# Attention and a squared-ReLU feed-forward on one core: three quarters of the up tiles in seven block products, two merged unit queues, banks taken late

## The chip, the cores and the metric

The kernel runs on one core of one Trainium2 chip. The metric is the device time of one execution in microseconds, taken as the median of several runs. A core has a matrix engine (PE in the profile; its weight loads are the separate row PEld), a vector engine (DVE), a scalar engine (ACT), a general engine (POOL) and a queue engine (SP); they run their own instruction streams in order and meet at semaphores.

## What is computed

Eight batches of grouped-query attention (16 query heads, 4 key/value heads, 384 tokens, head size 64) give 3072 tokens of width 1024. They go through a feed-forward block of width 2048 with a squared ReLU.

```python
batch, n_q_heads, n_kv_heads, seq, head_dim = (8, 16, 4, 384, 64)
scores = scale * np.matmul(q, k.transpose(0, 1, 3, 2))
attn = np.exp(scores)
attn = attn / (np.sum(attn, axis=-1, keepdims=True) + 1e-09)
attn_out = np.matmul(attn, v)
x = attn_out.transpose(0, 2, 1, 3).reshape(B * S, H * D)   # 3072 x 1024
h = np.maximum(x @ w_in, 0.0)                              # w_in 1024 x 2048
out = h * h @ w_out                                        # w_out 2048 x 1024
```

## The kernel before

A Python program writes out the instruction streams of all engines. `Recorder.add` (line 53) puts one operation on one engine, derives its semaphore waits from the names of what it reads and writes, and keeps an assumed start and end for it. From those assumed times the loop at lines 1109 to 1159 decides what TensorE does next. So the order on each engine is fixed before the launch, and an engine whose next instruction isn't ready simply stands.

The matrix array is used as two halves of 64 rows. A `Piece` (line 453) is one matmul over 64 rows, and two pieces on different halves run side by side. A unit of work is all pieces of the lower half followed, from the point that `hold_back` (line 465) sets, by all pieces of the upper half into the same PSUM bank. Four banks serve the feed-forward work (`F_BANKS`, line 501), three the scores, and one, `po`, the attention output.

The work of a batch has these kinds of unit:

- Scores (`row_scores`, line 512): for each pair of heads six matmuls of 384 columns, three to one exponential on ACT (line 524) into one of three `expT` buffers.
- Attention output (`row_attend`, line 535): 36 matmuls of 65 columns into `po`, then a reciprocal and a multiplication on DVE (lines 548 and 550) into `o_sb`, and a DMA transpose (`put_x`, line 433) into one of three `xT` buffers.
- Up tile (`row_up`, line 623): 128 of the 2048 hidden features for the 384 tokens of a batch. Eight pieces of 384 columns on each half, a ReLU on DVE (line 641) into one of three `hr` buffers, a square on ACT (line 649) into `h2T`. Sixteen tiles a batch, one after the other.
- Down products: the first two blocks of 128 tokens are plain (`row_down`, line 677). All others go in pairs of 128-token blocks, and each pair is done in seven products in place of eight (`product`, line 756; `p1` to `p3`, `rest`): sums of weight blocks are made once (`w_sums`, line 710), sums of activation blocks for every pair on DVE (`a_sums`, line 735). Product 1 and 2, and 5 and 3, share a PSUM bank and add up there.

The feed-forward is one stream of units (`feed_forward`, line 949: the up tiles of a batch, then its down pairs), and the attention another; the loop mixes them by a pace per batch (`PACE`, line 1006). Inputs of the next batch are loaded by POOL (`load_k`, `load_q`, `load_v`, lines 207 to 222): k and v land in `k_st` and `v_st`, POOL copies k twice into `k_dup` (line 354) and v into `v_aug` (line 383), and SP issues DMA transposes of k and q (`turn_k` and `turn_q`, lines 360 to 374).

```python
161 NEX, NXT, NHR, NY, NO, NS = 3, 3, 3, 6, 4, 5
592 ((load_k, 62000.0), (load_q, 67000.0), (load_v, 68500.0))
```

Line 161 holds the buffer counts; line 592 the assumed landing times of the third batch's loads, in ns, which the planner uses for that batch alone.

Of the kernel before, what the change touches and what calls it, by code (L numbers as in the profile page):

```python
# [9 lines left out]
class Recorder:  # L10
# [6 lines left out]
    def __init__(self, nc):  # L17
        self.nc = nc
        self.ops = []
        self.writer = {}  # L20
        self.readers = {}
        self.dma_sems = {}
        self.dma_last = {}
        self.idle_at = dict.fromkeys(self.ENGINES, 0.0)
        self.rows_at = [0.0, 0.0]
        self.stalled = {}
# [3 lines left out]

    def needs(self, eng, reads, writes, dma=None, after=()):
        deps = set()
# [9 lines left out]
        for d in deps:  # L42
            o = self.ops[d]
            if o["dma"] is None and o["eng"] == eng and dma is None:
                if eng in self.IN_ORDER or d not in raw:
                    continue
            need.add(d)
# [5 lines left out]
    def add(self, eng, fn, reads=(), writes=(), dma=None, after=(), ns=500.0, lat=2200.0, rows=None, end=None):  # L53
        i = len(self.ops)
        need = self.needs(eng, reads, writes, dma, after)
# [81 lines left out]
def bass_gqa_attention__then__ffn_squared_relu_kernel(  # L137
# [23 lines left out]
    NEX, NXT, NHR, NY, NO, NS = 3, 3, 3, 6, 4, 5  # L161

    R = Recorder(nc)

# [4 lines left out]
    warm = sb("warm", [128, 256])  # L169
# [10 lines left out]
    k_st = sb("k_st", [128, HKV, NJ, D])  # L180
    v_st = sb("v_st", [128, HKV, NJ, D])
    k_dup = [a_late[:, 0:2 * NKV].rearrange("p (a x d) -> p a x d", a=HKV * NJ, x=2), sb("k_dup1", [128, HKV * NJ, 2, D]).ap()]
    EARLY_W = [("q_f", c) for c in range(NPB)] + [("k_f", g) for g in range(HKV)] + ["v_f"] + [("q_st", 0, c) for c in range(NPB)]
    EARLY_A = [("k_dup", 0, g, j) for g in range(HKV) for j in range(NJ)]
    q_st = [q_b0, q_next.ap()]
    v_aug = [sb(f"v_aug{i}", [128, HKV * NJ, D + 1]) for i in range(2)]
    kT = [sb(f"kT{i}", [128, HKV, S]) for i in range(2)]
    qT = [sb(f"qT{i}", [128, NPB, S]) for i in range(2)]
    expT = [sb(f"expT{i}", [128, 2 * NJ, S]) for i in range(NEX)]
    rinv = [sb(f"rinv{i}", [128, NJ, 2], f32) for i in range(2)]  # L190
    o_sb = [sb(f"o_sb{i}", [128, NJ, 2, D]) for i in range(NO)]
    xT = [sb(f"xT{i}", [128, NKC, S]) for i in range(NXT)]
    w_in_sb = sb("w_in_sb", [128, NKC, FF], f16)
    w_out_sb = sb("w_out_sb", [128, NFC, F], f16)
    hr = [sb(f"hr{i}", [128, S], f32) for i in range(NHR)]
    h2T = [sb(f"h2T{i}", [128, NFC, S]) for i in range(2)]
    y_sb = [sb(f"y_sb{i}", [128, F // 2], f32) for i in range(NY)]

# [8 lines left out]
    def load_k(b, after=(), end=None):  # L207
        R.add("gpsimd", lambda g: g.dma_start(
            k_st.ap().rearrange("p g j d -> p g (j d)"),
            k[b].rearrange("g (p j) d -> p g (j d)", j=NJ)),  # L210
            writes=["k_st"], dma="k", after=after, ns=900.0, lat=LOADS, end=end)

    def load_v(b, after=(), end=None):
        R.add("gpsimd", lambda g: g.dma_start(
            v_st.ap().rearrange("p g j d -> p g (j d)"),
            v[b].rearrange("g (p j) d -> p g (j d)", j=NJ)),
            writes=["v_st"], dma="v", after=after, ns=900.0, lat=LOADS, end=end)
# [9 lines left out]
    def load_w_in(i):  # L227
        R.add("gpsimd", lambda g: g.dma_start(
            w_in_sb[:, :, i * WC:(i + 1) * WC],
            moe_w_in[:, i * WC:(i + 1) * WC].rearrange("(c p) f -> p c f", p=128)),  # L230
            writes=[("w_in", i)], dma=f"wi{i}", end=20500.0 + 2700.0 * i)
# [13 lines left out]
    def first_q(c0, c1):  # L245
# [14 lines left out]
    R.add("vector", lambda e: e.memset(warm[:], 0.0), writes=["warm"])  # L260
# [3 lines left out]
        pattern=[[-1, 128]], channel_multiplier=1), reads=["ident"], writes=["ident"])  # L264
    for i in range(2):
# [6 lines left out]
    def dup_k(g, eng, j0=0, j1=NJ):  # L272
        src = k_f[:, g, j0:j1].unsqueeze(2).to_broadcast([128, j1 - j0, 2, D])
        R.add(eng, lambda e: e.tensor_copy(k_dup[0][:, g * NJ + j0:g * NJ + j1], src),
              reads=[("k_f", g)], writes=[("k_dup", 0, g, j) for j in range(j0, j1)])
# [43 lines left out]
    def turn_bank(banks):  # L319
        i = banks[slots[0] % len(banks)]  # L320
        slots[0] += 1
        if i >= 5:
            return f_ps[i - 5].ap().bitcast(bf16)[:, 0:S], ("f_ps", i - 5)
        return sc_bf[:, i, 0:S], ("sc", i)

    def turn_on_pe(src, src_keys, dst, dst_keys, banks, eng="vector", n=NJ):
        ps, key = turn_bank(banks)

        def tr(pe):
            for t in range(n):  # L330
                m = pe.matmul(ps[:, t * 128:(t + 1) * 128], src[:, t * 128:(t + 1) * 128], ident[:],  # L331
# [3 lines left out]
        R.add("tensor", tr, reads=[*src_keys, "ident"], writes=[key])  # L335
# [4 lines left out]

    def first_kT(g, b=0, banks=RING, j0=0, j1=NJ):
        turn_on_pe(k_dup[b][:, g * NJ + j0:g * NJ + j1].rearrange("p a x d -> p (a x d)"),
                   [("k_dup", b, g, j) for j in range(j0, j1)], kT[b][:, g, j0 * 128:j1 * 128],
                   [("kT", b, g, j) for j in range(j0, j1)], banks, n=j1 - j0)

    def first_qT(c, b=0, banks=RING):
        turn_on_pe(q_st[b][:, 2 * c:2 * c + 2, :].rearrange("p h e -> p (h e)"), [("q_st", min(b, 1), c)],
                   qT[b][:, c], [("qT", b, c)], banks)

    def first_oT(c, banks=RING, eng="vector"):  # L350
        turn_on_pe(o_sb[c % NO].ap().rearrange("p i s d -> p (i s d)"), [("o_sb", c % NO, x) for x in range(2)],
                   xT[0][:, c], [("xT", 0, c)], banks, eng)

    def dup_all_k(b, eng="vector"):
        src = k_st.ap().rearrange("p g j d -> p (g j) d").unsqueeze(2)
        R.add(eng, lambda e: e.tensor_copy(
            k_dup[1][:, :, :, :], src.to_broadcast([128, HKV * NJ, 2, D])),
            reads=["k_st"], writes=[("k_dup", 1, g, j) for g in range(HKV) for j in range(NJ)], ns=1500.0)

    def turn_k(b, g):  # L360
        gs = slice(g * NJ, (g + 2) * NJ)
        R.add("sync", lambda e: e.dma_start_transpose(
            kT[b % 2][:, g:g + 2].rearrange("p g (j c) -> p (g j) c", j=NJ),
            k_dup[1][:, gs].rearrange("p a x d -> p (a x d)")),
            reads=[("k_dup", 1, x, j) for x in (g, g + 1) for j in range(NJ)],
            writes=[("kT", b % 2, x, j) for x in (g, g + 1) for j in range(NJ)], dma=f"kt{b % 2}_{g}", ns=1250.0)

    def turn_q(b, c):
        cs = (c, c + 1)
        R.add("sync", lambda e: e.dma_start_transpose(  # L370
            qT[b % 2][:, c:c + 2, :].rearrange("p h (t c) -> p (h t) c", t=NJ),
            q_st[1][:, 2 * c:2 * c + 4, :].rearrange("p h e -> p (h e)")),
            reads=[("q_st", 1, x) for x in cs], writes=[("qT", b % 2, x) for x in cs],
# [9 lines left out]
    def prepare_v(b):  # L383
        R.add("gpsimd" if b > 1 else "vector", lambda e: e.tensor_copy(
            v_aug[b % 2][:, :, 0:D], v_st.ap().rearrange("p g j d -> p (g j) d")),
            reads=["v_st"], writes=[("v_aug", b % 2)])

    def operands(p):
        b, c = p // NPB, p % NPB
        return kT[b % 2][:, c // 2], qT[b % 2][:, c], [("qT", b % 2, c)], [("kT", b % 2, c // 2, j) for j in range(NJ)]  # L390
# [18 lines left out]
    def attend(p, s, alone=False):  # L409
        b, g = p // NPB, (p % NPB) // 2  # L410
        acc, acc_key = (po_alt, ("sc", 1)) if alone and s == 1 else (po_v, "po")

        def av(pe):
            for i in range(NJ):
                f = NJ * s + i
                for j in range(NJ):
                    m = pe.matmul(acc[:, i, s, :], expT[p % NEX][:, 2 * j + f % 2, f // 2 * 128:f // 2 * 128 + 128],  # L417
                                  v_aug[b % 2][:, g * NJ + j, :], start=(j == 0), stop=(j == NJ - 1))
# [14 lines left out]
    def put_x(p):  # L433
# [4 lines left out]
            reads=[("o_sb", p % NO, x) for x in range(2)], writes=[("xT", b % NXT, c)], dma=f"xt{p % 8}", ns=1250.0)  # L438

    GAP = 450.0  # L440
    START = 30000.0
    behind = []
# [22 lines left out]
    def hold_back(hi, last, done, frees=()):  # L465
        job = dict(hi=list(hi), ready=R.ops[last]["start"] + GAP, after=[last], done=done, over=False, frees=frees)
        behind.append(job)
        return job

    def next_hi():  # L470
        job = behind[0]
        op = job["last"] = job["hi"].pop(0).emit(job["after"])
        job["after"] = ()
        if not job["hi"]:
            behind.pop(0)
            job["over"] = True

            def finish():
                free.extend(job["frees"])
                if job["done"]:  # L480
                    job["done"]()

            at(R.ops[op]["end"], finish)
# [5 lines left out]
    def push(kind, lo, hi, done=None, prev=None, frees=()):  # L489
        if prev is not None:  # L490
            yield from wait(lambda: prev["over"])
        after = [prev["last"]] if prev is not None else ()
        for piece in lo:
            if piece.test:
                yield from wait(piece.test)
            last = yield kind, piece, after
            after = ()
        return hold_back(hi, last, done, frees)

    ROWS = (slice(0, 64), slice(64, 128))  # L500
    F_BANKS = [(sc_ps[:, 3], ("sc", 3)), (sc_ps[:, 4], ("sc", 4)), (f_ps[0].ap(), ("f_ps", 0)), (f_ps[1].ap(), ("f_ps", 1))]
    free = [0, 1, 2, 3]

    def next_bank():
        yield from wait(lambda: free)
        return free.pop(0)

    exped, scaled = set(), {NPB - 1}
    voiced = {1}
    turned, usable, upped = {}, {0}, set()  # L510

    def row_scores(p, half):
        kt, qt, keys, k_keys = operands(p)
# [8 lines left out]
        def over(last):  # L522
            def exp():
# [9 lines left out]
        return [piece(i) for i in range(3)], over, lambda: before in exped and parts <= prepared  # L533

    def row_attend(p, then=None):
        b, g = p // NPB, (p % NPB) // 2

        def piece(r, f, j):
            rows = ROWS[r]
            return Piece(r, 33.0, lambda pe: pe.matmul(  # L540
                po_v[:, f % NJ, f // NJ, :], expT[p % NEX][rows, 2 * j + f % 2, f // 2 * 128:f // 2 * 128 + 128],
                v_aug[b % 2][rows, g * NJ + j, :], start=(r == 0 and f == 0 and j == 0), stop=(r == 1),
                skip_group_check=True),
                [("expT", p % NEX, 2 * j + f % 2), ("v_aug", b % 2), ("v_one", b % 2)], ["po"])

        def done():
            rinv_v = rinv[p % 2].ap().unsqueeze(3)
            R.add("vector", lambda e: e.reciprocal(rinv_v, po_v[:, :, :, D:D + 1]),
                  reads=["po"], writes=[("rinv", p % 2)], ns=200.0)
            op = R.add("vector", lambda e: e.tensor_tensor(o_sb[p % NO][:, :, :, :], po_v[:, :, :, 0:D],  # L550
                                                           rinv_v.to_broadcast([128, NJ, 2, D]), ALU.mult),
                       reads=["po", ("rinv", p % 2)], writes=[("o_sb", p % NO, x) for x in range(2)], ns=560.0)
# [7 lines left out]
            if turned[b] == NPB:  # L560
                usable.add(b)
# [3 lines left out]
        lo, hi = ([piece(r, f, j) for f in range(2 * NJ) for j in range(NJ)] for r in range(2))  # L565
# [625 lines left out]
```

The softmax here doesn't subtract the row's maximum and nothing guards it: scores larger than these inputs give would overflow.

## Time and profile before

| | |
|---|---|
| median of 3 runs | 415.98 us (415.8 to 416.05) |
| the profiled execution | 416.05 us |
| its span in the profile | 414.2 us |
| PE busy | 406.9 us, 98% |
| DVE busy / ACT busy / POOL busy | 216.1 / 216.2 / 53.7 us |
| granted TensorE clock | 1.0 |
| data moved by DMA | 44.26 MB in 93353 packets |

The span is what the profile covers, and 1.85 us of the execution lie around it. Busy time of PE counts a matmul from its start to its modelled end, while the next ones already stream behind it, so 98% says only that PE had always something in flight. How much of the array was used has to be counted from the spacing of the starts.

### The profile page before, as it was taken

What the parts mean: (1) busy time and instruction counts of PE and PEld (TensorE: products, weight loads), DVE (VectorE), ACT (ScalarE), POOL (GpSimd) and SP (SyncE); (2) the same over time, 40 slices, a digit from 0 to 9 for tenths busy, and PEclk for the clock granted to TensorE, in tenths of its full rate; (3) what the DMA queues carried; (4) which work ended last, traced back from release to release, by engine and by line L of the source; (5) the groups of instructions that cost most, each with busy time, mean ns of one, the idle gap of its engine ahead of it and who ended that gap; (6) DMA issues with size and microseconds to landing.
All of it is one profiled execution on the core that took longest, in us unless ns stands there. A gap on an engine that the chain in (4) does not pass through costs nothing.

```text
span 414.2 us, 13446 instructions
## 1 busy us (share of the span) xinstructions
PE 406.9 (98%) x6129; PEld 312.3 (75%) x6129; DVE 216.1 (52%) x480; ACT 216.2 (52%) x282; POOL 53.7 (13%) x68
## 2 busy tenths in 40 slices
PE   7999999999999999999999999999999999999997
PEld 4656776777767888778876799778877786788774
DVE  2664551469845466246556445535655446435553
ACT  4885762775655564655645466655664453213200
POOL 5852211041012000300003000300000000000000
PEclk9999999999999999999999999999999999999999
DMA  8999995657859841966029960698112210020012
GB/s 231 198 197 202 208 202 86 122 71 96 143 142 158 182 69 29 113 142 119 21 60 141 181 135 13 56 179 152 17 47 97 98 47 11 2 103 2 27 77 103
DMA packets 93353, 44.26 MB, mean 107 GB/s; under 512 B 71664, under 2 KB 87280, under 8 KB 93296
## 3 DMA queue, kind: packets, MB, share of 16 engines
q0 software_dynamic: 34288, 16.65, 31.8%
q1 hardware_dynamic: 55968, 24.49, 27.6%
q10 hardware_dynamic: 3040, 2.26, 1.8%
q8 instruction: 48, 0.79, 0.8%
q14 instruction: 9, 0.07, 0.1%
HBM read 35.65 MB, written 12.58 MB: 116 GB/s over the span
## 4 chain that ended last, share of the span: by engine, by line
PE 94%; DMA 3%; DVE 2%; ACTq 0%; issue 0%; ACT 0%; POOL 0%; DVEq 0%
PE f_ps L630 20%; PE sc_ps L630 17%; PE f_ps L794 16%; PE sc_ps L794 15%; PE po L540 12%; PE sc_ps L519 6%; PE sc_ps L688 2%; DMA w_late<-in_q_dram 2%; PE f_ps L688 2%; PE po L417 1%; PE sc_ps L400 1%; DMA xT<-o_sb 1%; DVE o_sb L430 1%; PE sc_ps L331 0%; PE f_ps L331 0%; PE sc_ps L577 0%
## 5 line engine op out<-in xcount | busy, mean ns | idle before, releaser
L630 PE MATMUL f_ps<-xT,w_in_sb 64*128 64x384 bf16 x1040 | 171.6, 322 | 0.0
L630 PE MATMUL sc_ps<-xT,w_in_sb 64*128 64x384 bf16 x992 | 168.9, 323 | 0.2 <-DMA xT<-o_sb 0.2
L524 ACT ACTIVATE expT<-sc_ps 128x1152 bf16<-128x1152 f32 x110 | 124.2, 1129 | 81.2 <-PE sc_ps L519 55.3
L630 PEld LDWEIGHTS f_ps<-xT,w_in_sb 64*128 64x128 f16 x1040 | 89.8, 94 | 14.3
L649 ACT ACTIVATE h2T<-hr 128x384 bf16<-128x384 f32 x121 | 62.4, 520 | 67.7 <-DVE hr L641 67.0
L630 PEld LDWEIGHTS sc_ps<-xT,w_in_sb 64*128 64x128 f16 x992 | 87.8, 94 | 12.3 <-DMA xT<-o_sb 0.3
L540 PEld LDWEIGHTS po<-v_aug,expT 64*128 64x128 bf16 x2016 | 78.1, 94 | 15.1 <-DVE o_sb L550 2.0
L540 PE MATMUL po<-v_aug,expT 64*128 64x65 bf16 x2016 | 85.0, 190 | 0.0
L794 PE MATMUL f_ps<-w_out_sb,h2T 64*128 64x512 f16 x240 | 60.5, 376 | 0.0
L794 PE MATMUL sc_ps<-w_out_sb,a_late 64*128 64x512 f16 x240 | 59.8, 376 | 0.0
L519 PE MATMUL sc_ps<-qT,kT 64*128 64x384 bf16 x330 | 56.3, 323 | 0.0
L794 PE MATMUL sc_ps<-w_late,h2T 64*128 64x512 f16 x224 | 55.9, 376 | 0.0
L641 DVE TENSOR_SCALAR hr<-f_ps 128x384 f32<-128x384 f32 x65 | 36.1, 556 | 36.7 <-PE f_ps L630 27.0
L641 DVE TENSOR_SCALAR hr<-sc_ps 128x384 f32<-128x384 f32 x62 | 34.2, 556 | 35.6 <-PE sc_ps L630 21.4
L702 DVE TENSOR_TENSOR y_sb<-sc_ps,y_sb 128x512 f32<-128x512 f32 (+1 forms) x31 | 21.2, 687 | 47.1 <-PE po L540 23.4
L550 DVE TENSOR_TENSOR o_sb<-po,rinv 128x384 bf16<-128x384 f32 x56 | 31.2, 557 | 1.9
L794 PE MATMUL f_ps<-w_late,a_late 64*128 64x512 f16 x128 | 32.1, 376 | 0.0
L794 PE MATMUL f_ps<-w_late,h2T 64*128 64x512 f16 x128 | 31.8, 376 | 0.0
L519 PEld LDWEIGHTS sc_ps<-qT,kT 64*128 64x128 bf16 x330 | 24.5, 94 | 6.8 <-ACT expT L524 0.4
L794 PEld LDWEIGHTS sc_ps<-w_out_sb,a_late 64*128 64x128 bf16 x240 | 22.1, 94 | 4.8 <-PE f_ps L794 0.3
L794 PEld LDWEIGHTS f_ps<-w_out_sb,h2T 64*128 64x128 bf16 x240 | 21.5, 94 | 5.4 <-PE f_ps L630 0.2
L794 PEld LDWEIGHTS sc_ps<-w_late,h2T 64*128 64x128 bf16 x224 | 20.5, 94 | 6.0 <-PE sc_ps L794 0.2
(104 smaller groups left out, 407.8 us busy)
## 6 DMA issues: line engine op xcount, KB each, us to landing
out_dram<-y_sb SPq DMA_DIRECT2D x47, 256.0 KB, 2.5
q_next<-in_q_dram POOLq DMA_DIRECT2D x7, 768.0 KB, 11.3
w_in_sb<-in_moe_w_in_dram POOLq DMA_DIRECT2D x8, 512.0 KB, 11.8
w_out_sb<-in_moe_w_out_dram POOLq DMA_DIRECT2D x2, 2048.0 KB, 32.1
k_st<-in_k_dram POOLq DMA_DIRECT2D x7, 192.0 KB, 4.6
v_st<-in_v_dram POOLq DMA_DIRECT2D x7, 192.0 KB, 11.8
w_late<-in_q_dram ACTq DMA_DIRECT2D x1, 768.0 KB, 9.8
xT<-o_sb SPq DMA_TRANSPOSE x48, 2.6
```

What stands on the lines that cost most here:

```text
L400: m = pe.matmul(sc_ps[:, 2 * u + x, 0:S], kt[rows, j * 128:(j + 1) * 128], qt[rows, :])
L417: m = pe.matmul(acc[:, i, s, :], expT[p % NEX][:, 2 * j + f % 2, f // 2 * 128:f // 2 * 128 + 128], v_aug[b % 2][:, g * NJ + j, :], start=( ...
L519: return Piece(x, 162.5, lambda pe: pe.matmul(sc_ps[:, i, 0:S], kt[rows, j * 128:(j + 1) * 128], qt[rows, :]), keys + k_keys[j:j + 1], [(" ...
L524: R.add("scalar", lambda e: e.activation(expT[p % NEX][:, 3 * half:3 * half + 3, :], sc_ps[:, 0:3, 0:S], AF.Exp, scale=0.125), ns=1130.0, ...
L540: return Piece(r, 33.0, lambda pe: pe.matmul(po_v[:, f % NJ, f // NJ, :], expT[p % NEX][rows, 2 * j + f % 2, f // 2 * 128:f // 2 * 128 + 128],
L550: op = R.add("vector", lambda e: e.tensor_tensor(o_sb[p % NO][:, :, :, :], po_v[:, :, :, 0:D], rinv_v.to_broadcast([128, NJ, 2, D]), ALU.m ...
L630: return Piece(h, 162.5, lambda pe: pe.matmul(acc[:, 0:S], w_in_sb[rows, kc, c * 128:(c + 1) * 128], xT[b % NXT][rows, kc, :], start=(h == ...
L641: op = R.add("vector", lambda e: e.tensor_scalar_max(hr[r][:, :], acc[:, 0:S], 0.0), reads=[key], writes=[("hr", r)], ns=560.0)
L649: op = R.add("scalar", lambda e: e.activation(h2T[b % 2][:, c, :], hr[r][:, :], AF.Square), reads=[("hr", r)], writes=h2(b, c), ns=520.0)
L688: return Piece(h, 216.0, lambda pe: pe.matmul(acc, h2T[b % 2][rows, c, i * 128:(i + 1) * 128], w_out_sb[rows, c, jj * 512:(jj + 1) * 512], ...
L702: return R.add("vector", lambda e: e.tensor_tensor(out_ap, a, b, op), reads=reads, writes=writes, ns=ns)
L794: return Piece(h, 216.0, lambda pe: pe.matmul(acc, lhs[rows], right[rows, c], start=(first and h == 0 and c == 0), stop=(h == 1 and c == N ...
```

## The change

The up tiles of batches 2 to 7 are treated as the down products already were. `UPG = (0,1,2)` names three of four groups; a group is two neighbouring tiles and their two partners eight tiles on. Its input is split in two halves of the 1024 inputs, two halves of the 384 tokens (192 each) and two halves of the features, and its output is made of seven products, each of which holds two tiles of 192 tokens in one bank (`up_product`). The fourth group keeps `row_up`. Four sums of `xT` blocks per batch are made on DVE (`x_sums`), three sums of weight blocks per group on POOL (`u_sums`), and a fourth of them in place. What a bank holds goes through f32 buffers (`y_sb`, which also take the place of `hr`): product 1 is copied by ACT, the six others give seven DVE additions, and ReLU and square are then two ACT instructions.

In the down pairs `EA` and `GA` put products 1 and 2, and 5 and 3, in banks of their own, with a DVE addition for the sum. Up units and down units are now two streams (`up_stream`, `down_stream`); the loop starts the unit that can begin first, and a unit may begin on either half of the array. A bank is taken when a unit's first matmul is sent (`Place`), and `po` joins the common banks. `expT` and `xT` have two buffers in place of three, `kT` and `qT` one and a half batches in place of two. k is loaded by two DMAs straight into `k_dup`, v straight into `v_aug`. Same-engine dependencies on DVE, ACT and POOL are now always waited for (`needs`).

```diff
-    NEX, NXT, NHR, NY, NO, NS = 3, 3, 3, 6, 4, 5
+    NEX, NXT, NY, NO, NS = 2, 2, 7, 4, 6
+    UPG = (0,1,2,)
+    NG, HT, KH = len(UPG), S // 2, NKC // 2
...
     def load_k(b, after=(), end=None):
-        R.add("gpsimd", lambda g: g.dma_start(
-            k_st.ap().rearrange("p g j d -> p g (j d)"),
-            k[b].rearrange("g (p j) d -> p g (j d)", j=NJ)),
+        for x in range(2):
+            R.add("gpsimd", lambda g, x=x: g.dma_start(
+                k_dup[1][:, :, x, :], k[b].rearrange("g (j p) d -> p (g j) d", j=NJ)),
...
     def load_v(b, after=(), end=None):
         R.add("gpsimd", lambda g: g.dma_start(
-            v_st.ap().rearrange("p g j d -> p g (j d)"),
+            v_aug[b % 2][:, :, 0:D], v[b].rearrange("g (j p) d -> p (g j) d", j=NJ)),
...
+    def x_sums(b, which):
...
+            if n == 1:
+                op = tensor_op(x_sum[s1], A21, A22, ALU.add, k21 + k22, k1 + EARLY_A, ns)
+            if n == 2:
+                op = tensor_op(x_sum[s2], x_sum[s1], A11, ALU.subtract, k1 + k11, k2 + EARLY_A, ns)
+            if n == 3:
+                op = tensor_op(x_s3[:, :, :], A11, A21, ALU.subtract, k11 + k21, ["x_s3"], ns)
+            if n == 4:
+                op = tensor_op(x_sum[s4], A12, x_sum[s2], ALU.subtract, k12 + k2, k4 + EARLY_A, ns)
...
+    def u_sums(g, n, eng="gpsimd", behind=()):
...
+        if n == 3:
+            x = op(T[3][0], V22, V12, ALU.subtract, k22 + k12, T[3][1])
+        if n == 2:
+            x = op(T[2][0], T[3][0], V11, ALU.add, T[3][1] + k11, T[2][1])
+        if n == 4:
+            x = op(T[4][0], T[2][0], V21, ALU.subtract, T[2][1] + k21, T[4][1])
+        if n == 1:
+            x = op(V12, V12, V11, ALU.subtract, k12 + k11, k12)
...
+    def up_product(q, n, bank, first, done, prev=None, frees=()):
...
+        def piece(h, second, e, kc):
+            rows = ROWS[h]
+            w, wk = weight(kc, e)
+            x, k = moving(kc)
+            return Piece(h, 82.5, lambda pe: pe.matmul(bank.acc[:, e * HT:(e + 1) * HT], w[rows], x[rows],
...
+        parts = [lambda r, second: [piece(r, second, e, kc) for e in range(2) for kc in range(KH)]]
...
+    def relu_square(b, c, half, y, then, eng):
...
+            R.add("scalar", lambda e: e.activation(y_sb[y][:, 0:S], y_sb[y][:, 0:S], AF.Relu), reads=[("y", y)],
+                  writes=[("y", y)], ns=520.0)
+            op = R.add("scalar", lambda e: e.activation(dst, src, AF.Square), reads=[("y", y)], writes=keys, ns=520.0)
...
+            lead, ahead, behind = MIX
+            yield from some(lead)
+            for g in UPG:
+                u = dict(b=b, g=g, hook=pump)
+                yield from up_p1(u)
+                yield from some(ahead)
+                yield from up_p2(u)
+                for p in (up_p6, up_p7, up_p5, up_p4):
+                    yield from p(u)
+                yield from some(behind)
+                yield from up_p3(u)
+            yield from some(NFC)
...
+    EA, GA, UA, UZ = (True, True, True, True)
...
-    ffn, att = all_feed_forward(), attention()
+    att = attention()
...
+    streams = [up_stream(), down_stream()]
```

## The prediction

> **What bounds the kernel now.** I read the page first (busy shares, then groups), then the order of time on PE, then what PE waits for, and last the few places where another engine holds something up.
>
> ```profile
> PE 406.9 (98%) x6129; PEld 312.3 (75%) x6129; DVE 216.1 (52%) x480; ACT 216.2 (52%) x282; POOL 53.7 (13%) x68
> PE   7999999999999999999999999999999999999997
> ...
> L630 PE MATMUL f_ps<-xT,w_in_sb 64*128 64x384 bf16 x1040 | 171.6, 322 | 0.0
> L630 PE MATMUL sc_ps<-xT,w_in_sb 64*128 64x384 bf16 x992 | 168.9, 323 | 0.2 <-DMA xT<-o_sb 0.2
> L524 ACT ACTIVATE expT<-sc_ps 128x1152 bf16<-128x1152 f32 x110 | 124.2, 1129 | 81.2 <-PE sc_ps L519 55.3
> ...
> L641 DVE TENSOR_SCALAR hr<-f_ps 128x384 f32<-128x384 f32 x65 | 36.1, 556 | 36.7 <-PE f_ps L630 27.0
> ```
>
> PE is never idle, DVE and ACT are half idle and wait for PE. But a busy PE isn't a full array; the spacing of starts tells that. From the timeline, PE alone, at 372 us and at 32.5 us:
>
> ```profile
> 372.04 0.32 PE L630 MATMUL f_ps<-xT,w_in_sb 64*128 64x384 bf16 x1
> 372.12 0.32 PE L630 MATMUL sc_ps<-xT,w_in_sb 64*128 64x384 bf16 x1
> 372.20 0.32 PE L630 MATMUL f_ps<-xT,w_in_sb 64*128 64x384 bf16 x1
> ...
> 32.60 0.19 PE L577 MATMUL sc_ps<-ident,q_next 64*128 64x64 bf16 x1
> 32.62 0.19 PE L577 MATMUL f_ps<-ident,q_next 64*128 64x64 bf16 x1
> 32.63 0.19 PE L577 MATMUL sc_ps<-ident,q_next 64*128 64x64 bf16 x1
> ```
>
> The two halves of the array take turns; each starts a 384-column matmul every 0.162 us, so both together one every 0.081 us. In the same way a 512-column one (L794) costs 0.216 us on its half, 0.108 us of the array, and a 65-column one (L540) about 0.032 us on its half, 0.016 us of the array. The 64-column ones start every 10 to 20 ns on alternating halves, weight loads included.
>
> With these spacings all work after 31.8 us (where the half-row matmuls begin) is: L630 2032 x 0.081 = 165.1, L794 1216 x 0.108 = 131.3, L688 128 x 0.108 = 13.8, L519 330 x 0.081 = 26.8, L540 2016 x 0.016 = 32.3, L577 1.2, the last product L781 1.7: 372.2 us. The last matmul ends near 411.6 us, 379.8 us after 31.8. So only 7.6 us of the array are unused there: some 3 us between 30 and 40 us, about 1 us near 163 us where an up tile waits for an `xT` transpose, about 1 us at the tail, the rest in crumbs. The kernel is bound by columns through the array.
>
> **What the Trainium skill says.** "TensorE: Matmul & The Clock Gate", section Back-to-back issue gap, gives N/2.4 + 2.5 ns for a lone stream; for 384 and 512 columns that is 162.5 and 215.8, which the trace has (0.162, 0.216). The same section warns that at small N weight loads set a longer spacing; the 10 to 20 ns starts above don't show it in this use of halves. "TensorEngine Tiling (Array Packing)", section PSUM Bottleneck, says that tiling speeds up TensorE and not the emptying of PSUM, which may become the bottleneck. This trace has it hidden so far (DVE 52%). "SBUF — State Buffer", section Who interferes with whom, says that a DVE instruction with two SBUF inputs and a GpSimd one that reads SBUF lock each other out for a whole instruction. The trace agrees:
>
> ```profile
> 222.39 1.63 DVE L702 TENSOR_TENSOR a_late<-h2T,a_late 128x1024 bf16<-128x1024 bf16 x1
> ...
> 222.01 1.47 POOL L356 COPY k_dup<-k_st 128x1536 bf16<-128x1536 bf16 x1 [1.95 <-DMA k_st<-in_k_dram]
> ```
>
> The DVE sum takes 1.63 us in place of 0.68 beside a POOL copy. "DMA: Bandwidth & Descriptors", section Why small descriptors are slow (HBM only), says that each packet has a fixed cost; used below.
>
> **The change part by part, in array time.** In six batches 12 of 16 up tiles go: 6 x 12 x 16 = 1152 half-row matmuls x 0.081 = 93.6 us. Added are 6 x 3 groups x 7 products x 16 = 2016 matmuls of 192 columns. The trace has no such width. Between its neighbours (0.0325 for 65, 0.162 for 384; slope 0.418 ns a column between 384 and 512) it comes to 82.3 ns on a half, 0.0412 of the array: 83.0 us. From both sides: 80 ns is bare streaming by that slope, and 2.5 to 5 ns more on each gives 85 to 87.5 ns or 86 to 88 us. I take 83.0, so **-10.6 us** (bounds -5.5 to -13). Weight loads double per column, but 41 ns between starts is more than the 10 to 20 ns seen.
>
> All other matmuls stay: scores, attention outputs and down products have the same counts in the changed program.
>
> *DVE.* Less: 72 ReLUs x 0.556 = 40.0. More: 7 additions x 18 groups = 126 x 0.558 (the 384-column addition in the group of L702) = 70.3; 24 `x_sums` of 768 columns, between 0.42 (512) and 0.68 (1024), 0.55 each: 13.2; 17 additions more in the down pairs (`EA`, `GA`) x 0.69 = 11.7. Sum +55, 216 to 271 us, 66% of the span. *ACT.* 72 ReLUs x 0.52 = 37.4, 18 copies x 0.52 = 9.4, 7 copies fewer x 0.58: +43, to 259 us. Neither bounds the whole. Locally they are near it: an up product is 16 x 0.0412 = 0.66 us of array, and costs 0.56 us of DVE and (2 x 4 + 1) x 0.52 / 7 = 0.67 us of ACT, where a tile was 1.3 us of array to 0.56 and 0.52. In stretches with many up products beside exponentials (1.13 us a half pair) ACT wants about all of the time. Down products (1.73 us of array to 0.69 us of DVE) from the other stream fill in, and five banks and seven `y_sb` let evacuation run late. Price: a stretch in which ACT or DVE is asked for 5% more than there is, some 10 us in each of six batches, would lose 0.5 us each if nothing filled in: 3 us; I take +1.5 (0 to 6).
>
> *POOL.* `k_dup` and `v_aug` copies go (14 us). Twelve `u_sums` of 1024 columns come; the nearest row is the POOL product L646, 384 columns in 0.83 us, so about 2.2 us each, 26 us, in the stretch of 75 to 110 us beside the DVE sums. Each meeting can hold a DVE sum for up to 2.2 us as above; banks cover most of it. +0.5 (0 to 3).
>
> *DMA.* A k load was 512 packets of 384 bytes; now it is 2 x 1536 of 128 bytes, and v 1536 in place of 512. In the trace's packet records, software-queue packets of 384 bytes take 51 ns, 512 bytes 60 ns, 1024 bytes 98 ns on one of 16 engines; that line gives about 32 ns at 128 bytes, and the queue moves some 1.4 times what these times say: 1.4 ns a packet. k and v grow by 4 us a batch (bounds 1.3 and 7). In later batches the load starts some 30 us ahead of its first use, and 4 us is hidden. At the beginning it isn't: that queue is full from 10 to 65 us, with `w_in`, `w_out` and the third batch's inputs behind each other, and the order waits for exactly these:
>
> ```profile
> 61.83 1.46 POOL L356 COPY k_dup<-k_st 128x1536 bf16<-128x1536 bf16 x1 [3.83 <-DMA k_st<-in_k_dram]
> ...
> 71.62 1.27 SPq L370 DMA_TRANSPOSE qT<-q_next  x1
> ...
> 74.98 0.48 PE L519 MATMUL sc_ps<-qT,kT 64*128 64x384 bf16 x3
> ```
>
> k lands at 61.8, q and v by 67 us; the q transpose takes 3.3 us to land, at 74.9, and the first scores start at 74.98. The assumed times (62, 67, 68.5) are unchanged. In the new order the array work ahead of those scores ends near 71.2 us plus the 3 us of early gaps, about 74.5. With k and v of the second batch and k of the third in front, q lands 4 + 3 us later, near 73; transposes at 73 and 74.4 land at 77.7. Scores are in order on PE, so everything behind them stands: 3 us, 0 to 6 with the bounds. As part of it may be taken up by the early gaps, +2.0. `w_in` chunks keep 5 us and more of slack; one DMA more to issue on POOL ahead of the first casts costs +0.3 (0 to 1.5).
>
> *Merged streams and late banks.* The gaps near 163 us and in the crumbs can now be filled by units of the other stream: -0.8 (0 to -2.5). Two `xT` and `expT` buffers in place of three act the other way, within the 1.5 above: attention of a batch may not write `xT` until the up units two batches before are over, and the order has down units to send meanwhile. Same-engine waits end when the engine's last instruction does; no cost on PE.
>
> Sum: 414.2 - 10.6 + 1.5 + 0.5 + 2.0 + 0.3 - 0.8 = 407.1 us of span, with 1.85 around it 408.95, against the profiled execution's 416.05. That stands 0.07 above the median, so **408.9 us**.
>
> **Rivals.**
> - *More than that (403).* No give-back, gaps filled: 414.2 - 10.6 - 2.5 + 1.85 = 403. For it: PE waits for nothing else today. Against: the q transpose above already lands just as it is used.
> - *Little is left (414.5).* Loads at the upper bound (+6) and ACT/DVE stretches at +3: 414.2 - 10.6 + 9 + 1.85 = 414.5. For it: both margins are thin in this trace.
> - *Slower (423.5): evacuation sets the pace.* In every batch's up stretch banks aren't emptied as fast as products end, because DVE also has sums and attention outputs queued in order and ACT exponentials. 3 us lost in each of six batches: +18, 414.2 - 10.6 + 18 + 1.85 = 423.5. It decides from 10.6 / 6 = 1.8 us a batch. For it: 0.56 and 0.67 us of work to 0.66 us of array. Against: a batch is some 46 us of array work, for which DVE has about 35 us (25 additions and ReLUs 13.9, `x_sums` 2.2, attention 6.0, down additions 7.3, `a_sums` 5.7) and ACT about 35 (exponentials 18.1, squares, ReLUs and copies 17).
> - *It doesn't save array time.* If a 192-column matmul took 93 ns on its half, 2016 of them would cost the 93.6 us saved. The 64- and 65-column rows speak against such a floor; I count it with the third case.
>
> **How the numbers follow.** Forecast 0.55, more 0.15, little left 0.12, slower 0.18. The forecast's own range is 405 to 412. Without the slower case, and cut at the edges, 402.5 to 417 holds some 8 in 10. A change of 0.2% (0.8 us) is about what this kernel's runs can tell from none. Faster: 0.55 + 0.15 + 0.09 of the third; same 0.03 of it; slower 0.18.
>
> **What would show it.** Right: 192-column matmuls starting 41 ns apart on alternating halves; PE groups for up work near 154 us of array time in place of 165; DVE near 270 and ACT near 260 us; the first scores of the third batch with a wait of 1 to 4 us for a `qT` or `kT` transpose. Wrong: PE idle before up products, released by DVE additions on `y_sb` or ACT, in every batch (the slower case); 192-column starts over 45 ns apart; no wait near 75 us (the loads cost nothing).

## The result and the profile after

The changed kernel takes 427.62 us (median of 4 runs, 426.08 to 428.8), the kernel before 415.89 us beside it. The ratio is 1.028, 95% interval 1.0245 to 1.0321: slower by 2.8%, where 408.9 us had been forecast. The profiled execution took 428.8 us with a span of 426.3.

From the page of the kernel after, the busy times, then PE and the granted clock in 40 slices of 10.7 us:

```profile
PE 406.8 (95%) x6993; PEld 316.6 (74%) x6993; DVE 277.2 (65%) x573; ACT 253.1 (59%) x365; POOL 75.6 (18%) x76
...
PE   7989999894899999999999999999999999999997
...
PEclk9999999986999999999999999999999999999999
```

PE was at 9 throughout before. Now there is a hole in the eighth to eleventh slice, 75 to 117 us, and the clock falls in the same place. Most of the loss is local, then, and the rest of the row tells nothing, as a busy PE isn't a full array. So I count as the prediction did: the starts after 32 us, each by the array time of its width, taken from the time between 32 us and the last start. This unused array time was 6.4 us before and is 28.9 us after; the work itself fell from 373.0 to 362.5 us. (The level shifts by about 1 us with the array time taken for the smallest matmuls, which is why the prediction has 7.6 us; the differences don't.) The two differences, +22.5 and -10.5, are the 12.1 us by which the span grew. Of the 22.5 us, 15.0 lie between 80 and 120 us (15.6 us unused, 0.6 before), and 7.5 are spread over the rest.

What stands in the hole is read from the timeline of DVE after (start, duration, line, operation, out<-in):

```profile
92.17 2.39 DVE L1015 TENSOR_TENSOR a_late<-h2T 128x384 bf16<-128x384 bf16 x1 [0.59 <-ACT h2T L760]
94.60 2.15 DVE L1015 TENSOR_TENSOR a_late<-a_late,h2T 128x384 bf16<-128x384 bf16 x1
96.68 2.27 DVE L1015 TENSOR_TENSOR h2T<-h2T 128x384 bf16<-128x384 bf16 x1
98.87 2.27 DVE L1015 TENSOR_TENSOR a_late<-h2T,a_late 128x384 bf16<-128x384 bf16 x1
101.06 0.54 DVE L752 TENSOR_SCALAR y_sb<-f_ps 128x384 f32<-128x384 f32 x1
...
105.43 2.17 DVE L1015 TENSOR_TENSOR a_late<-a_late,h2T 128x128 bf16<-128x128 bf16 x1
```

the timeline of POOL:

```profile
92.18 2.16 POOL L840 TENSOR_TENSOR u_late<-u_late,w_in_sb 128x1024 f16<-128x1024 f16 x1
94.26 2.27 POOL L840 TENSOR_TENSOR u_late<-w_in_sb 128x1024 f16<-128x1024 f16 x1
96.61 4.31 POOL L840 TENSOR_TENSOR u_late<-u_late,w_in_sb 128x1024 f16<-128x1024 f16 x2
```

and that of PE:

```profile
94.64 0.38 PE L996 MATMUL f_ps<-w_out_sb,h2T 64*128 64x512 f16 x1
101.66 0.40 PE L622 MATMUL f_ps<-v_aug,expT 64*128 64x65 bf16 x4 [6.65 <-DVE y_sb L752]
```

A sum of 384 columns takes 0.36 us on DVE when it is alone, and one of 128 columns 0.22 us. Here both take 2.2 us, which is the length of one `u_sums` instruction on POOL, and the sum's width no longer matters. The four `a_sums` of a pair follow each other, each beside the next POOL sum, so from 92.2 to 101.1 us DVE finishes four small sums and empties no bank. PE starts its last matmul at 94.64 us, 2.5 us after the first of them began, and stands for 6.65 us until the ReLU at L752 has given a bank back. The row of PE names the ReLU, which took 0.54 us; what held it is the queue in front of it.

The loss goes on after PE restarts. From the windows of the kernel after (PE busy and count, PEld, DVE, ACT, POOL, then the granted clock):

```profile
86.00:87.00 1.00, 1.00 (x8) 0.67 (x6) 0.00 (x0) 0.24 (x1) 0.00 (x0) 0.50 0.00 0
103.00:104.00 1.00, 1.00 (x8) 0.45 (x6) 0.38 (x1) 0.59 (x2) 0.92 (x2) 0.50 0.44 94
```

PE is busy all of each window and starts only 8 matmuls in it; the clock is at 0.5. By the trace's clock records it stays there from 84.55 to 87.96 us, after a stand of 1.94 us (behind one DVE sum that took 2.23 us), and until 105.03 us after the long one, with PE at work again from 101.66. That is 6.8 us of work at half speed, about 3.4 us of array.

### The profile page after: what moved, and what is told of

It reads as the page before. It is cut to its first block, busy times and chain, and to the rows that moved or that the text cites. A ratio compares the mean times of both kernels' runs of the same rounds, so it can differ in the third digit from the quotient of the medians.

```text
span 426.3 us, 15417 instructions
## 1 busy us (share of the span) xinstructions
PE 406.8 (95%) x6993; PEld 316.6 (74%) x6993; DVE 277.2 (65%) x573; ACT 253.1 (59%) x365; POOL 75.6 (18%) x76
## 4 chain that ended last, share of the span: by engine, by line
PE 88%; DVE 8%; ACT 2%; issue 1%; DMA 1%; DVEq 0%
PE f_ps L1098 13%; PE sc_ps L1098 10%; PE sc_ps L890 9%; PE f_ps L890 8%; PE sc_ps L744 6%; PE sc_ps L592 6%; PE sc_ps L622 6%; PE f_ps L744 6%; PE po L1098 5%; PE po L890 4%; DVE a_late L1015 4%; PE po L744 3%; PE f_ps L622 3%; PE po L622 2%; PE sc_ps L412 1%; PE f_ps L996 1%
## 5 line engine op out<-in xcount | busy, mean ns | idle before, releaser
L744 PE MATMUL sc_ps<-xT,w_in_sb 64*128 64x384 f16 x336 | 64.6, 329 | 1.9 <-DVE o_sb L634 1.9
L744 PE MATMUL f_ps<-xT,w_in_sb 64*128 64x384 f16 x336 | 65.1, 326 | 0.2 <-DVE y_sb L1310 0.2
L1098 PE MATMUL f_ps<-w_late,h2T 64*128 64x512 f16 x208 | 51.2, 376 | 0.0
L787 ACT ACTIVATE y_sb<-y_sb 128x384 f32<-128x384 f32 x72 | 37.3, 518 | 22.6 <-DVE y_sb L1015 21.5
L622 PEld LDWEIGHTS sc_ps<-v_aug,expT 64*128 64x128 bf16 x1008 | 37.2, 94 | 8.5 <-PE po L744 1.3
L1098 PE MATMUL f_ps<-w_out_sb,h2T 64*128 64x512 f16 x176 | 43.1, 376 | 0.0
L622 PE MATMUL sc_ps<-v_aug,expT 64*128 64x65 bf16 x1008 | 41.6, 190 | 1.1 <-issue 0.7
L760 ACT ACTIVATE h2T<-y_sb 128x384 bf16<-128x384 f32 x49 | 25.6, 522 | 28.5 <-DVE y_sb L752 28.1
L744 PE MATMUL po<-xT,w_in_sb 64*128 64x384 f16 x208 | 41.5, 323 | 0.0
L225 POOL DMA_DIRECT2D k_dup<-in_k_dram x14 | 14.5, 1045 | 147.9 <-DMA xT<-o_sb 147.9
L1098 PE MATMUL f_ps<-w_out_sb,a_late 64*128 64x512 f16 x160 | 39.5, 376 | 0.0
L789 ACT ACTIVATE h2T<-y_sb 128x384 bf16<-128x384 f32 x72 | 37.7, 523 | 2.3
L744 PEld LDWEIGHTS sc_ps<-xT,w_in_sb 64*128 64x128 f16 x336 | 29.5, 96 | 8.0 <-DVE o_sb L634 2.3
L744 PEld LDWEIGHTS f_ps<-xT,w_in_sb 64*128 64x128 f16 x336 | 29.7, 95 | 3.3 <-DVE y_sb L1310 0.4
L1098 PE MATMUL sc_ps<-w_late,h2T 64*128 64x512 f16 x128 | 31.0, 376 | 0.0
## 6 DMA issues: line engine op xcount, KB each, us to landing
w_in_sb<-in_moe_w_in_dram POOLq DMA_DIRECT2D x8, 512.0 KB, 14.5
```

The source lines that it names most:

```text
L225: R.add("gpsimd", lambda g, x=x: g.dma_start(k_dup[1][:, :, x, :], k[b].rearrange("g (j p) d -> p (g j) d", j=NJ)), writes=[("k_dup", 1, g ...
L622: return Piece(r, 33.0, lambda pe: pe.matmul(place[1][:, f % NJ, f // NJ, :], expT[p % NEX][rows, 2 * j + f % 2, f // 2 * 128:f // 2 * 128 ...
L744: return Piece(h, (t1 - t0) / 2.4 + 2.5, lambda pe: pe.matmul(place.acc[:, t0:t1], w_in_sb[rows, kc, c * 128:(c + 1) * 128], xT[b % NXT][r ...
L760: op = R.add("scalar", lambda e: e.activation(h2T[b % 2][:, c, :], y_sb[y][:, 0:S], AF.Square), reads=[("y", y)], writes=h2(b, c), ns=520.0)
L787: R.add("scalar", lambda e: e.activation(y_sb[y][:, 0:S], y_sb[y][:, 0:S], AF.Relu), reads=[("y", y)], writes=[("y", y)], ns=520.0)
L789: op = R.add("scalar", lambda e: e.activation(dst, src, AF.Square), reads=[("y", y)], writes=keys, ns=520.0)
```

## Experiments

Theory: the twelve weight sums on POOL lock the DVE sums out one by one, and this is the loss. Rival: evacuation can't keep up with the products in any batch, wherever the sums are made.

**The sums on DVE.**

```diff
-            op = u_sums(*todo[0], behind=behind)
+            op = u_sums(*todo[0], eng="vector", behind=behind)
```

> The changed kernel with its twelve sums of up-weight blocks moved from POOL to DVE (0.69 us each, 8.3 us in all). Theory A (POOL sums and DVE sums of two SBUF inputs lock each other out, DVE falls behind between 78 and 112 us, PE stands): the 15 us lost there come back less 1 to 3 us for the added DVE work, 411 to 414 us, and the DVE sums of 128 to 512 columns take 0.2 to 0.45 us again. Theory B (DVE and ACT have too much work and banks are emptied late, wherever the sums are made): DVE gets more, so no better than 424 us.

Measured: 414.95 us, ratio to the kernel before 0.9956 (0.9931 to 0.9981). From its page:

```profile
PE 403.7 (98%) x6993; PEld 315.1 (76%) x6993; DVE 266.8 (65%) x585; ACT 253.0 (61%) x365; POOL 50.0 (12%) x64
...
PEclk9999999999999999999999999999999999999999
```

DVE has taken over twelve sums of 0.68 us and is busy for 10.4 us less than in the kernel after. The hole is gone (2.7 us unused between 80 and 120 us) and the clock is full. Moving 8 us of work onto the busier engine brought 12.7 us. The time is 1 us above the upper end expected, so something else still takes most of the array's saving.

**The same sums on POOL in quarters.** Is it the POOL work, or the length of one of its instructions?

```diff
-            return R.add(eng, lambda e: e.tensor_tensor(o, a, b, op), reads=r, writes=w, ns=ns, after=behind)
+            for c in range(KH):
+                x = R.add(eng, lambda e, c=c: e.tensor_tensor(o[:, c:c + 1], a[:, c:c + 1], b[:, c:c + 1], op), ...)
```

> The changed kernel with each of the twelve POOL sums cut into four of 256 columns. Theory A with a lock held for a whole instruction: a DVE sum waits at most about 0.55 us where it waited 2.2, so most of the 15 us go: 415 to 420 us. If POOL and DVE shared bandwidth instead, the same POOL work would slow DVE by the same total: 425 to 429 us. Theory B: no change, 427 us.

Measured: 415.16 us, ratio 0.9968 (0.995 to 0.9985). POOL's busy time rises to 85.2 us, and DVE's falls to 264.5. From the timelines of DVE and POOL:

```profile
93.66 0.59 DVE L1018 TENSOR_TENSOR a_late<-a_late,h2T 128x128 bf16<-128x128 bf16 x1
```

```profile
93.51 2.91 POOL L841 TENSOR_TENSOR u_late<-w_in_sb 128x256 f16<-128x256 f16 x4
```

A 128-column sum now takes 0.59 us and not 2.17, beside POOL instructions of 0.73 us (2.91 / 4). A DVE sum waits for one POOL instruction, however much POOL has to do; had the two shared bandwidth, POOL's unchanged work would have kept the time near 427 us.

**POOL sums in the kernel before.** Twelve POOL additions whose results nobody uses are put into the kernel before, near 101 us, and in a second kernel twenty POOL fills in the same place.

```diff
+        for n in range(12):
+            R.add("gpsimd", lambda g: g.tensor_tensor(out, w_in_sb[:, 0:4, 0:192], w_in_sb[:, 4:8, 0:192], ALU.add), ...)
...
+        for n in range(20):
+            R.add("gpsimd", lambda g: g.memset(out, 0.0), ...)
```

> The kernel before, with twelve POOL additions of 768 columns (two SBUF inputs, result into a staging buffer that nobody reads then; nothing of the computation changes) between about 102 and 122 us, where DVE makes its sums of weights. All other engines have the same order. Theory A: DVE sums beside them take about 1.7 us in place of 0.7, PE loses 3 to 10 us, 419 to 426 us. Theory B: 416 us.

> As the run before, but POOL fills the staging buffer with zeros twenty times (about 1 us each) in place of the additions: it writes SBUF and reads nothing. Theory A, lock on the read interface alone: 416 us, DVE sums at 0.7 us. If any POOL work at that point cost time (its later loads, the write side), it would be as slow as the run with additions.

Measured: 425.18 us with the sums, ratio 1.0191 (1.0132 to 1.025), and 416.38 us with the fills (one run; the kernel before had 416.29 us as median beside it). From the timelines of DVE, the sums first, then the fills:

```profile
104.15 4.05 DVE L702 TENSOR_TENSOR w_late<-w_late,w_out_sb 128x1024 f16<-128x1024 f16 x2
```

```profile
103.21 1.42 DVE L702 TENSOR_TENSOR w_late<-w_late,w_out_sb 128x1024 f16<-128x1024 f16 x2
```

Two sums take 4.05 us beside POOL additions and 1.42 us beside POOL fills. The array time goes where the additions are: 9.3 us unused between 100 and 130 us, against 0.6 in the kernel before. So nothing else of the change is needed for the loss, and a POOL instruction that reads no SBUF doesn't cause it.

**What became of the 10.6 us.** With the sums on DVE the array has 10.6 us less to do than before, and the kernel is only 1 us faster. Is it the new order of units, or the products? The first kernel here has no products, the second two groups, the fourth spreads the sums on DVE out; the third, with two groups, tests the loads, since 128-byte packets fill the queues where PE stood for "issue" (time in which it waited for nothing that the profile shows). All of them make the sums of `w_in` that are left on DVE.

```diff
-    UPG = (0,1,2,)
+    UPG = ()
...
-    UPG = (0,1,2,)
+    UPG = (0,1,)
...
-    def load_k(b, after=(), end=None):
+    def direct_k(b, after=(), end=None):
...
+    def load_k(b, after=(), end=None):
+        R.add("gpsimd", lambda g: g.dma_start(
+            k_st.ap().rearrange("p g j d -> p g (j d)"),
+            k[b].rearrange("g (p j) d -> p g (j d)", j=NJ)),
...
-            at(R.ops[op]["end"] - 200.0, lambda: all_u_sums(todo[1:]))
+            at(R.ops[op]["end"] + 1200.0, lambda: all_u_sums(todo[1:]))
```

> The changed kernel with no group of up tiles in block products (no group in the list, no sums of x and of w_in), everything else of the change kept: the merged unit queues, the banks taken late, the direct loads of k and v. Array work after 32 us goes back from 362.5 to 373.0 us. Theory P (the new scheduler costs the later stretch some 6 to 8 us, whatever runs in it): 415.0 of the run with the sums on VectorE plus 10.6 = 424 to 427. Theory Q (the scheduler is as good as the old one, and the products themselves bring the idle array, through more additions and more units): 414 to 418, as before.

> The changed kernel with the sums of w_in on VectorE and two groups of up tiles in products instead of three. A group is worth 3.5 us of array work (10.6 / 3). If what the third group saves reaches the end, 418 to 419, against 415.0 with three; if it is eaten by its additions and units, 414.5 to 416.

> As the kernel with two products, and from batch 2 on k and v are loaded as in the kernel before, into staging buffers in packets of 384 bytes, and copied by VectorE (one copy for k, one for v, some 0.5 to 1.5 us each per batch, six batches); SBUF of the third group's sums holds the staging buffers. Theory R (the 128-byte packets delay TensorE's instructions, about one gap of 0.7 to 1.5 us per batch and half-empty stretches around it): 2 to 5 us less than with two products and direct loads. Rival: the gaps are something else, and the time is the same or up to 2 us longer, by the copies on VectorE.

> The changed kernel with the sums of w_in on VectorE (three groups), but each sum set 1.2 us after the one before it ended instead of directly behind it, so that 12 sums of about 0.7 us take some 23 us and not 8. If what is left of the loss between 80 and 130 us (some 3 us of array time) comes from VectorE being closed to other work by the run of sums, 413 to 414; if the sums' total or something else makes it, 414.7 to 415.5, and over 415.5 if the later sums hold up the first products.

Measured: 414.71 us without products, ratio 0.9954 (0.9933 to 0.9975); 416.54 us with two, 0.9999 (0.9974 to 1.0024); 418.24 us with two and staged loads, 1.004 (1.002 to 1.006); 416.18 us with the sums spread, 0.9986 (0.9963 to 1.001). The rest of the change, the new order of units among it, is sound: without products it is a little faster than the kernel before. The products bring the idle array along. The staged loads made it slower and not faster, and PE still stands for "issue" once, for 1.0 us, in their trace, so packet size isn't what PE stood for. Spreading the sums didn't help either: 416.18 us lies where the later sums were expected to hold up the first products, and why stays open.

The stops for "issue" themselves are real but small. In the waits of PE with the sums on DVE:

```profile
PE sc_ps L622 <- issue: 1.3, 1, 1.3
```

The trace's records of the queue that brings PE its instructions show a fetch of 16 KB at 123.46 us and the next at 132.82, with 204 matmuls started in between, where some 130 go to a fetch; PE stopped at 133.8. With the sums spread there were 244 matmuls between two fetches and a stop of 2.3 us. The kernel before had 202 between the same two fetches and didn't stop, and 228 passed without a stop between two later fetches of the run with the sums on DVE. That PE had run out of instructions fits the stops but isn't shown, and why the fetch is late there wasn't tested.

**Banks or DVE.** Two theories remained. K: a product keeps the array busy for 0.66 us where a tile took 1.3, and holds a bank until its addition all the same, so that banks run short and halves of the array wait at the ends of units. D: the additions themselves are too much for DVE. One bank fewer, with and without products, and fewer additions with banks held longer (with `UA` and `UZ` off, product 2 adds up in the bank of product 1, and 3 in that of 5); the last run has one group:

```diff
-    free = [0, 1, 2, 3, 4]
+    free = [0, 1, 2, 3]
...
-    EA, GA, UA, UZ = (True, True, True, True)
+    EA, GA, UA, UZ = (True, True, False, False)
...
-    UPG = (0,1,2,)
+    UPG = (0,)
```

> The changed kernel with the sums of w_in on VectorE (three products) and one PSUM bank fewer to hand out: four for up tiles, products, down units, turns and attention, not five. Theory K (a product holds a bank for a short piece of array work and a long way to its addition, so that the units of the products are short of banks, and halves of the array wait at unit ends): the loss grows much more with products than without them, to 425 to 440, at least 10 us over 415.0, while the kernel without products with four banks stays within 8 us of its 414.7. Theory D (VectorE's additions themselves set the pace): about the same growth with and without products, 2 to 8 us in both.

> The kernel without products with one PSUM bank fewer to hand out, four and not five. Theory K: 416 to 422, since a tile of 16 matmuls of 162 ns keeps the array busy for 1.3 us per bank, twice as long as a product. Theory D: as much longer than 414.7 as the kernel with products becomes longer than 415.0 by the same loss.

> The changed kernel with the sums of w_in on VectorE, in which the second product of a group is summed by the array into the bank of the first, and the third into the bank of the fifth, as the down products of the kernel before do for some pairs: 36 additions of 128x384 fewer on VectorE (2 x 3 groups x 6 batches, 0.56 us each, 20 us of 267), but two banks of a group are held from one product to the next. Theory D: 1 to 5 us less than 415.0. Theory K: 2 to 10 us more.

> The changed kernel with the sums of w_in on VectorE and one group of up tiles in products instead of three. Its array work is 3.5 us less than with none. If each group loses in idle halves what it saves, 414 to 416.5, like none, two and three; if the first one is nearly free and the loss comes with several in a row, 411 to 413.5, and this would be the best version.

| | time, us | ratio to before (interval) | array work, us | unused, us |
|---|---|---|---|---|
| no products | 414.71 | 0.9954 (0.9933 to 0.9975) | 373.6 | 5.7 |
| one group | 417.14 | 1.0021 (1.0012 to 1.003) | 369.3 | 10.8 |
| two groups | 416.54 | 0.9999 (0.9974 to 1.0024) | 365.7 | 13.6 |
| three groups, sums on DVE | 414.95 | 0.9956 (0.9931 to 0.9981) | 362.4 | 15.4 |
| no products, four banks | 421.18 | 1.0113 (1.0097 to 1.0129) | 372.7 | 11.6 |
| three groups, four banks | 436.88 | 1.0494 (1.0473 to 1.0516) | 362.8 | 38.2 |
| three groups, fewer additions | 422.31 | 1.0139 (1.0117 to 1.0161) | 362.5 | 22.3 |

(Array work and unused time as above: after 32 us, from one trace each, whose time isn't the median: 416.03 us for no products.) One bank fewer costs 6.5 us without products and 21.9 us with them. Taking 36 additions off DVE, with busy time down from 266.8 to 250.6 us, made the kernel 7.4 us slower. Both are as K has it, and the last contradicts D as the main cause. From none to three groups the unused time rises step by step, by 9.7 us in all, about what the array saves; the times of one and two groups, 1.6 to 2.4 us above those of none and three, were not foreseen and are not explained.

How such time looks, from the timeline of PE with three groups and the sums on DVE, then those of PE's weight loads and of DVE:

```profile
279.13 0.24 PE L890 MATMUL po<-xT,w_in_sb 64*128 64x192 f16 x1
279.13 0.24 PE L890 MATMUL sc_ps<-xT,w_in_sb 64*128 64x192 f16 x1
279.21 0.65 PE L744 MATMUL sc_ps<-xT,w_in_sb 64*128 64x384 f16 x3
279.92 0.25 PE L890 MATMUL f_ps<-a_late,u_late 64*128 64x192 f16 x1
```

```profile
279.92 0.09 PEld L890 LDWEIGHTS f_ps<-a_late,u_late 64*128 64x128 f16 x1 [0.45 <-DVE o_sb L634]
```

```profile
279.31 0.56 DVE L634 TENSOR_TENSOR o_sb<-f_ps,rinv 128x384 f16<-128x384 f32 x1
```

Up to 279.2 us both halves have work. Then only L744 starts for 0.7 us, on one half. The other half's next product goes to `f_ps`, which an attention output holds until DVE has scaled it at 279.87 us. PE counts as busy throughout, and its own waits don't show it; only the row of its weight load does. At other places the second half of a unit stands for the end of its first. Here it is a down product (L1098), whose last matmul on one half starts at 293.48 us and whose first on the other at 293.91:

```profile
293.05 0.81 PE L1098 MATMUL f_ps<-w_late,h2T 64*128 64x512 f16 x3
293.69 0.41 PE L890 MATMUL sc_ps<-a_late,w_in_sb 64*128 64x192 f16 x3
293.91 0.39 PE L1098 MATMUL f_ps<-w_late,h2T 64*128 64x512 f16 x1
```

An up product has half a tile's array time, so such ends come about twice as often; what they cost in all wasn't counted.

How the 9.7 us divide between banks, the order of halves and late instructions stays open. No version tried is below 414.7 us; three beat the kernel before, by 0.3 to 0.5% (0.3% by the medians), and one of them has no products at all.

## Why the prediction was wrong

- **The POOL sums: this step failed.** "Each meeting can hold a DVE sum for up to 2.2 us as above; banks cover most of it. +0.5 (0 to 3)." The mechanism was right, and so was the size of one meeting. It is what the Trainium skill's "SBUF — State Buffer", section Who interferes with whom, says of two-input DVE instructions and GpSimd reads, and of an instruction that only writes; 2.15 us beside a sum and unchanged times beside fills agree. Wrong was the cover. The banks covered 2.5 us, once, not 2.2 us at every meeting: four sums in a row meet four POOL sums, 8.9 us in which nothing is emptied. 15.6 us of array went unused between 80 and 120 us, about 3.4 of them by the half clock, which no term had. With the sums on DVE the kernel is 12.7 us faster.
- **The array's work** was right: 10.5 us less in the traces, 10.6 predicted. Its working had a slip: the straight line between 65 and 384 columns gives 84.1 ns on a half, not 82.3, and so -8.9 us; 82.3 is near what the slope of 0.418 ns gives from 384 columns down (81.7). That number was the better one: the 192-column starts are 41 ns apart, as in this row of the kernel after, (0.86 - 0.24) / 15:

```profile
282.18 0.86 PE L890 MATMUL f_ps<-xT,w_in_sb 64*128 64x192 f16 x16
```

- **"ACT/DVE stretches" (+1.5) and "merged streams fill gaps" (-0.8)** were +0.7 together and came out near +7.5 (by which the unused time outside 80 to 120 us grew). Banks were named as the cushion that lets evacuation run late; the runs with one bank fewer show them to be short. The busy times look near, ACT with 253.1 against 259, DVE with 277.2 against some 271, but the latter is luck: with the sums on DVE it is 266.8 us, 8.2 of them for these sums. So DVE's own work was 258.6 us, and some 18 us of the 277.2 were time that sums stood waiting beside POOL.
- **The late loads (+2.0)** cost nothing. The first k transpose went out at 64.07 us and the first q transpose at 68.19, a few us earlier than reckoned, and the array was full between 70 and 80 us. The sign that was to show it, a wait near 75 us, isn't there. The time of a 128-byte packet was right (32 ns in the packet records after).
- **The rival on the slower side** had the right sign and engine and the wrong shape. It asked for 3 us in each of six batches. There were some 15 us in one place by a lock, and about 1.2 us a batch (7.5 / 6) elsewhere, less than the 1.8 us from which it would have decided.

Put together on the predicted span of 407.1: +14.5 for the sums, +6.8 for the stretches, -2 for the loads give 426.4, against 426.3 measured. These terms are read from the same trace, so the sum shows that none is missing; it doesn't show the cause of the 6.8.

## What to carry to other kernels

Where an in-order engine meets a lock several times in a row, add the waits up and set the sum against the buffers' cover once, since nothing refills them in between; if another engine's helper work makes the lock, the busier engine may do it at less cost (8 us more to do left DVE 10 us less busy here). Before work is cut into smaller units, count what each unit holds from its first instruction to its release: seven products in place of four tiles, on the same five banks, idled about what they saved here.

## What was not expected of the hardware

- After PE had stood for only 1.9 us (81.41 to 83.35 us) the granted clock went to 0.5 for 3.4 us; with the sums spread, a stand of 2.3 us (133.85 to 136.12 us) left it full. The length of a stand alone doesn't decide. The Trainium skill's "TensorE: Matmul & The Clock Gate", section Part 1: The HAM clock gate, ties the half clock to an idle window of about 3.4 us and full speed to as long a busy one; the length of the slow stretch agrees (3.41 us and, counted from the restart after the stand of 6.65 us, 3.37 us), the idle time needed was shorter here.
- A DVE sum of 128 columns took 2.17 us beside 2.2 us POOL sums, ten times its 0.22 us, and 0.59 us beside POOL sums of a quarter the length.
